# Three tanh operations per head pair instead of four, in score tiles of two and of three PSUM banks, and gate exponentials as powers of e on GpSimd: a fused soft-capped attention and mixture-of-experts attention kernel

## The chip, the cores and the metric

The kernel runs on one core of one Trainium2 chip. The metric is the device time of one execution in microseconds (us); the number quoted for a version is the median of several executions. Beside it there is one profiled execution, from which all views below are taken.

## The reference

Two layers follow each other. The first is ordinary attention with a soft cap on the scores, for 8 batches, 12 heads, 448 tokens and 64 values per head. Its output, rearranged to 448 tokens by 768 features per batch, is the input x of the second layer: four small causal attention experts, of which each token uses the two with the largest gate logits.

```python
# layer 1, per batch and head (S = 448, head size 64, cap = 30)
scores = cap * tanh(q @ k.T / sqrt(64) / cap)
x = softmax(scores) @ v                      # heads side by side: (448, 768)

# layer 2, per batch (E = 4 experts, head size 64, top 2)
logits = x @ w_gate                          # (448, 4)
w = softmax over the two largest logits of each token
for e in range(4):
    a = causal_softmax((x @ wq[e]) @ (x @ wk[e]).T / 8)
    out += w_e * (a @ (x @ wv[e]) @ wo[e])   # only where e is among the two
```

The kernel leaves out the subtraction of the maximum: the cap bounds the scores, and the other exponents are small. Row sums come from a column of ones in v, and division comes after the product with v.

## The kernel before, in words

**Pairs.** Layer 1 is worked off in 48 pairs of heads (`NP`, six per batch). A pair needs, for 448 queries, seven blocks of 128 key rows by 448 query columns: chunk 0 is a block that both heads share (the last 64 keys of each, one head in the upper and one in the lower half of the rows), and chunks 1 to 3 are 128 keys each, once for each head. Seven blocks are 7 x 448 = 3136 columns per pair.

**Scores in PSUM.** A block of 448 f32 columns takes one PSUM bank of 512. The eight banks are split in two pools: `ps_score`, two tiles of two banks each, and `ps_aux`, four tiles of one bank, which everything else on TensorE shares (transposes, the products with v, all projections, the expert outputs). `fill` (L467) writes a score tile with matmuls (L476 for the shared block, L480 for the others, two of which run on half the rows of the array each), and `tanh` (L488) has ScalarE read it into the f16 tile y (L510). `HALF = (1, 2, 2, 2)` says how many blocks each of the four tanh operations of a pair takes. One exponential over all 3136 columns follows per pair (`expo`, L516). The last five pairs of the last batch are worked off in two halves of their tokens ("A" and "B", tiles s0A, s1A, s0B, s1B), so that the second layer of that batch can begin early.

**Second layer.** When the six pairs of a batch are done, its steps are queued: q and k of the experts (L724), v and gate logits (L640, with the copy of the logits at L663), scores (`b_fill`, L762, in the same score tiles), their exponentials on ScalarE (`b_exp`, L781) with the causal mask on GpSimd (L789), the product with v (L808), a transpose (L585), the output projection (L863) and the store (L884). `b_gexp` (L674) is the exponential of the gate logits, 128 x 16 values per batch, on ScalarE; its reader is the product `wun` on VectorE (L688).

**Order.** The list `prog` fixes the order on ScalarE: for a pair, its first tanh (T), the exponential (E) of the pair before, the other tanh operations, and in some slots two expert exponentials (X). `XAT` and `EXPB` say in which slots. All that read a score tile (T and X) are numbered; the fill of read n has to wait for read n - 2, which frees its tile. `Plan` is a planner that runs while the program is being written: it keeps a clock for TensorE, VectorE and ScalarE and a list of free aux banks, and puts the queued steps between the fills, as they become ready and by their due times. What it decides is fixed: each engine then executes its own list in order and waits on semaphores. `keep_warm` adds matmuls without use (L898) in the first 13 slots.

**The end.** `last_batch` takes what the planner has not yet placed, closes the score pool, opens its banks as a second pool for TensorE's outputs, and orders everything that remains with a search over a graph (`Graph`). GpSimd also casts the inputs (L385 to L404) and issues the weight loads; inputs and outputs go through SyncE's queue.

Of the kernel before, what the change touches and what calls it, by code (L numbers as in the profile page):

```python
# [10 lines left out]
f32 = mybir.dt.float32  # L11
f16 = mybir.dt.float16
AF = mybir.ActivationFunctionType
ALU = mybir.AluOpType
# [3 lines left out]
class Plan:  # L18
# [6 lines left out]
    def __init__(self):  # L25
        self.pe = self.dve = self.act = 0.0
        self.done = {}

        self.aux = [0.0] * 4
        self.opened = set()  # L30
        self.work = []

# [207 lines left out]
def kernel(  # L240
# [13 lines left out]
    nc = tc.nc  # L254

    B, H, S, Dh = q.shape
# [17 lines left out]
    xp = ctx.enter_context(tc.tile_pool(name="xp", bufs=2))  # L274
    bp = ctx.enter_context(tc.tile_pool(name="bp", bufs=2))
    outp = ctx.enter_context(tc.tile_pool(name="outp", bufs=8))
    ps_aux = ctx.enter_context(tc.tile_pool(name="ps_aux", bufs=4, space=bass.MemoryType.PSUM))
    scores = ctx.enter_context(ExitStack())
    ps_score = scores.enter_context(
        tc.tile_pool(name="ps_score", bufs=2, space=bass.MemoryType.PSUM)  # L280
    )

    ctx.enter_context(tc.manual_schedule())
# [154 lines left out]

    HALF = (1, 2, 2, 2)


    CUT = 256
# [4 lines left out]
    score = {}  # L449

    def fill_part(u, i):

        p, h = u
        qt, kt = qkt[p]
        x = slice(*TOK[h])
        n = x.stop - x.start
        sc = ps_score.tile([128, 2, 512], f32, name=f"s{i}{h}_{p}", tag="score")
        if i:
            nc.tensor.matmul(sc[:, 0, 0:n], kt[:, 0:128], qt[:, x], start=True, stop=True)
        for c in (2,) if i else (0, 1):  # L460
            for g in range(2):
                r = slice(64 * g, 64 * (g + 1))
                o = n * (1 - g) if i else n * c
                nc.tensor.matmul(
                    sc[:, g, o : o + n], kt[r, 128 * (c + 1) : 128 * (c + 2)], qt[r, x],
                    start=True, stop=True,
                )  # L467
        score[(u, i)] = sc

    def fill(p, i):  # L470
        if isinstance(p, tuple):
            return fill_part(p, i)
        qt, kt = qkt[p]
        sc = ps_score.tile([128, 2, 512], f32, name=f"s{i}_{p}", tag="score")
        if i == 0:
            nc.tensor.matmul(sc[:, 0, 0:S], kt[:, 0:128], qt, start=True, stop=True)  # L476
        else:
            for g in range(2):
                r = slice(64 * g, 64 * (g + 1))
                nc.tensor.matmul(  # L480
                    sc[:, g, 0:S], kt[r, 128 * i : 128 * (i + 1)], qt[r, :],
                    start=True, stop=True,
                )
        score[(p, i)] = sc

    y = {}
# [2 lines left out]
    def tanh(u, i):  # L489
        p, h = u if isinstance(u, tuple) else (u, "")  # L490
        if i == 0:
            y[u] = actp.tile([128, 7 * S], f16, name=f"y{h}_{p}", tag="y", bufs=2)
        sc = score.pop((u, i))
        if not h:
            o, n = sum(HALF[0:i]), HALF[i]
            parts = [(o * S, sc[:, 0:n, 0:S], n)]
        else:
            n = TOK[h][1] - TOK[h][0]
            if i == 0:
                parts = [(0, sc[:, :, 0 : 2 * n], 2)]  # L500
            elif 2 * n == 512:
                parts = [(4 * n, sc.rearrange("p b n -> p (b n)")[:, 0 : 3 * n], 1)]
            else:
                parts = [(4 * n, sc[:, 0, 0 : 2 * n], 1), (6 * n, sc[:, 1, 0:n], 1)]
        for o, src, k in parts:
            w = src.shape[-1]
            dst = y[u][:, o : o + k * w]
            if k > 1 or len(src.shape) > 2:
                dst = dst.rearrange("p (k w) -> p k w", w=w)
            nc.scalar.activation(dst, src, AF.Tanh, scale=isc / capf)  # L510
# [8 lines left out]
    def prob(p, w, j, g):  # L519

        h = "AB"[w >= CUT]
        if (p, h) in pr:
            lo, hi = TOK[h]
            i = (4 if j == 0 else 4 + g + (j == 3) if j > 2 else j - 1 + 2 * g)
            o = (hi - lo) * i + w - lo
            return pr[p, h][:, o : o + 128]
        o = S * (0 if j == 0 else 2 * j - 1 + g) + w
        return pr[p][:, o : o + 128]

    xt = {}  # L530
# [138 lines left out]
    def b_gexp(b, h=""):  # L669
        s = st[b]  # L670
        s["eexp", h] = bp.tile(
            [128, 2 if h else 4, E], f32, name=f"eexp{h}_{b}", tag="eexp", bufs=3
        )
        nc.scalar.activation(s["eexp", h], s["lg", h], AF.Exp)  # L674

    def gate_steps(b, h=""):

# [75 lines left out]
    def b_fill(b, r, g):  # L753
        s = st[b]
        qe = s["qe", r]
        ke = s["ke", r]
        sc = ps_score.tile([128, 1024], f32, name=f"sB{g}_{b}_{r}", tag="score")

        def block(e, o, ko, n, to):

            h = slice(64 * e, 64 * (e + 1))
            nc.tensor.matmul(  # L762
                sc[to : to + n, o : o + S - ko], ke[h, ko : ko + n], qe[h, ko:S], start=True,
                stop=True,
            )
# [192 lines left out]
    def rows(w):  # L958
        return w.rearrange("(c p) m -> p c m", p=128)

    loads = []
    for r in range(2):
        for e in (2 * r, 2 * r + 1):
# [7 lines left out]
        loads += [("o", wo2[e // 2][e % 2 * Dh : (e % 2 + 1) * Dh, :], moe_wo[e])]  # L971


    XAT = [(3, 5)] * 5 + [(2, 4), (2, 3), (3, 4)]
    EXPB = {HP * (b + 1) + o: (b, r) for b in range(B) for r, o in enumerate(XAT[b])}

    prog = []
    for i, u in enumerate(UNITS):  # L980
        t = [("T", u, k) for k in range(2 if isinstance(u, tuple) else 4)]
        e = [("E", UNITS[i - 1])] if i else []
        x = [("X", *EXPB[i], g) for g in range(1 if i >= NP else 2)] if i in EXPB else []
        prog.append(("S", i))
        if i in (1, 2):
            prog += e + t
        elif isinstance(u, tuple):
            prog += t[0:1] + e + x + t[1:]
        else:
            prog += t[0:1] + e + x[0:1] + t[1:2] + x[1:2] + t[2:4]  # L990
    prog += [("S", len(UNITS)), ("E", UNITS[-1])]
    reads = [o for o in prog if o[0] in "TX"]
    where = [i for i, o in enumerate(prog) if o[0] in "TX"]
# [4 lines left out]
    def dur(o):  # L998
        if o[0] == "S":
            return 0.0  # L1000
        if o[0] == "X":
            return 0.7 if o[1] == B - 1 else 0.9
        n = S
        if isinstance(o[1], tuple):
            n = TOK[o[1][1]][1] - TOK[o[1][1]][0]
        if o[0] == "E":
            return 0.08 + 0.00084 * 7 * n
        if n < S:
            return 0.05 + 0.00084 * n * (4, 3)[o[2]] + 0.04 * (o[2] == 1 and n < 256)
        return 0.055 + 0.373 * HALF[o[2]]  # L1010

    def fill_dep(o):
        if o[0] == "T":
# [5 lines left out]
    def do_fill():  # L1019
        nonlocal nfill  # L1020
        o = reads[nfill]
        rel = ends[nfill - 2] + 0.15 if nfill >= 2 else 0.0
        cost = 0.36 if o[0] == "X" or o[2] or isinstance(o[1], tuple) else 0.19
        for d in fill_dep(o):
            plan.force(d)
        at = plan.act + sum(dur(x) for x in prog[pos : where[nfill]])
        rel = max(rel, *(plan.done[d] for d in fill_dep(o)))
        plan.pump(rel, max(rel + 0.05, at - cost - 0.25))
        plan.pe = max(plan.pe, rel) + cost
        if o[0] == "T":  # L1030
# [194 lines left out]


    def l_fill(b, r, _):
        sc = ps_score.tile([128, 2, 512], f32, name=f"sLA_{r}", tag="score")
        o = 0
        for _, k0, q0, q1 in BANKS["A", r][0]:  # L1230
            for e in range(2):
# [8 lines left out]
    def l_exp(b, r, _):  # L1240
# [1 line left out]
        o = BANKS["A", r][1]  # L1242
        dst = pL[:, r, o : o + 768]
        nc.scalar.activation(
            dst.rearrange("p (e n) -> p e n", e=2), st[b].pop(("sc", r))[:, :, 0:384], AF.Exp,
            scale=isc,
        )
        for e in range(2):
# [6 lines left out]
    def last_batch():  # L1255
# [17 lines left out]
        G = Graph(  # L1273
            dict(PE=plan.pe, DVE=plan.dve, ACT=plan.act, SP=plan.act, DMA=plan.act),
            dict(aux=[(0.0, t) for t in plan.aux], tail=[(0.0, t3)] * 4),
        )

        BR, BA, BW, BX = 0.0, 0.0, -5.0, 0.0
# [319 lines left out]
    def gate_exp(wait=False):  # L1598
# [71 lines left out]
```

## Time and profile before

| quantity | value |
|---|---|
| median of 3 executions | 320.8 us (320.77 to 320.8) |
| profiled execution, its own time | 320.99 us |
| span of that execution, first to last instruction | 319.3 us |
| granted TensorE clock, mean | 0.987 |
| ScalarE (ACT) busy | 306.8 us, 96% |
| TensorE (PE) busy | 284.9 us, 89% |
| VectorE (DVE) busy | 216.8 us, 68% |
| GpSimd (POOL) busy | 157.1 us, 49% |

An engine's busy time is the time covered by its instructions. Instructions of ScalarE overlap: the next one begins before the one ahead of it has ended, so the mean duration of a group is longer than the time by which each of them moves the engine on. Waits are named as "who <- whom". Lines such as L510 are lines of the kernel before; in the changed kernel the same statements stand some 20 to 40 lines further down.

### The profile page before, as it was taken

The numbers are of one execution on the slowest core, as the hardware profiler recorded it, in microseconds if no ns is written. First come the engines' busy times: TensorE is split into PE (matmuls) and PEld (weight loads), VectorE is DVE, ScalarE is ACT, GpSimd is POOL, SyncE is SP. The second block draws the span as 40 slices with busy tenths as digits, with TensorE's granted clock in tenths as the row PEclk, the third lists the DMA queues.
The fourth block names the chain that finished last, engine by engine and source line by source line (L and its number), as shares of the span: only waits on it lengthen the run. The fifth ranks groups of instructions, "written<-read, shape, count | busy, mean of one in ns | idle before, by whom it ended". The sixth has DMA issues, their size and how long they took to land.

```text
span 319.3 us, 9111 instructions
## 1 busy us (share of the span) xinstructions
PE 284.9 (89%) x3445; PEld 179.6 (56%) x3445; DVE 216.8 (68%) x762; ACT 306.8 (96%) x312; POOL 157.1 (49%) x480
## 2 busy tenths in 40 slices
PE   7887879988999889997799899997999879989994
PEld 2454445655565655566556564655655655556762
DVE  4444446686686877678866876767856976577574
ACT  3999999999999999999999999999999999999973
POOL 4586999947607299865805386082905200220200
PEclk9999999999999999999999979999899999999999
DMA  7699999999026999576083945586012102020134
GB/s 163 173 216 241 211 225 214 223 216 230 4 101 170 257 243 275 148 214 161 13 242 95 257 95 150 169 218 157 3 52 99 27 2 102 0 77 2 52 123 175
DMA packets 65404, 46.22 MB, mean 145 GB/s; under 512 B 26000, under 2 KB 61968, under 8 KB 65360
## 3 DMA queue, kind: packets, MB, share of 16 engines
q1 hardware_dynamic: 54064, 43.28, 53.0%
q0 software_dynamic: 10512, 1.58, 7.1%
q10 hardware_dynamic: 784, 0.77, 0.8%
q8 instruction: 27, 0.44, 0.6%
q14 instruction: 17, 0.14, 0.2%
HBM read 36.19 MB, written 11.01 MB: 148 GB/s over the span
## 4 chain that ended last, share of the span: by engine, by line
ACT 78%; PE 12%; issue 7%; DMA 1%; DVE 1%; DVEq 0%; POOL 0%; ACTq 0%; POOLq 0%
ACT y L510 36%; ACT p L516 30%; ACT pBs L781 8%; PE wops L863 2%; PE vps L640 2%; DMA qf<-in_q_dram 1%; ACT yB L510 1%; PE pv L550 1%; PE qps L724 1%; ACT yA L510 1%; PE kps L724 1%; PE qkB L1171 1%; ACT pB L516 1%; PE pv L544 1%; ACT pBs L1479 0%
## 5 line engine op out<-in xcount | busy, mean ns | idle before, releaser
L510 ACT ACTIVATE y<-s 128x896 f16<-128x896 f32 (+1 forms) x172 | 135.5, 934 | 0.6 <-PE s L476 0.5
L516 ACT ACTIVATE p<-y 128x3136 f16<-128x3136 f16 x43 | 125.7, 2922 | 0.1
L789 POOL TENSOR_SCALAR_AFFINE_SELECT pBs<-pBs 128x128 f16<-128x128 f16 (+1 forms) x112 | 28.2, 277 | 103.5 <-ACT pBs L781 102.2
L550 PE MATMUL pv<-v16s,p 128*128 128x65 f16 x1032 | 55.0, 194 | 0.0
L480 PE MATMUL s<-qt,kt 64*128 64x448 f16 x258 | 46.5, 362 | 9.0 <-ACT y L510 6.8
L550 PEld LDWEIGHTS <-p 128*128 128x128 f16 x1032 | 46.6, 98 | 3.6 <-issue 0.4
L544 PE MATMUL pv<-vtzs,p 128*128 128x130 f16 x172 | 38.8, 225 | 9.0 <-ACT p L516 6.7
L559 DVE RECIPROCAL rc<-pv 128x4 f32<-128x4 f32 x96 | 17.3, 180 | 38.0 <-PE pv L550 36.8
L563 DVE TENSOR_TENSOR xk<-pv,rc 128x256 f16<-128x256 f32 x96 | 40.7, 424 | 3.2
L370 DVE COPY ob<-wops 128x384 f32<-128x384 f32 (+1 forms) x55 | 30.5, 554 | 6.3 <-PE wops L863 5.7
L544 PEld LDWEIGHTS <-p 128*128 128x128 f16 x172 | 16.7, 97 | 27.7 <-ACT p L516 15.5
L480 PEld LDWEIGHTS <-kt 64*128 64x128 f16 x258 | 15.7, 93 | 28.3 <-issue 21.5
L781 ACT ACTIVATE pBs<-sB 128x960 f16<-128x960 f32 (+1 forms) x28 | 30.9, 1116 | 0.5 <-PE sB L762 0.5
L863 PE MATMUL wops<-wo,oT 128*128 128x384 f16 x128 | 30.4, 327 | 0.6 <-DVE oT L370 0.4
L385 POOL CAST q<-qf 112x512 f16<-112x512 f32 x46 | 28.1, 611 | 4.7 <-DMA qf<-in_q_dram 2.8
L640 PE MATMUL vps<-wvg,xT 128*128 128x260 f16 (+1 forms) x192 | 29.6, 275 | 0.0
L399 POOL CAST v16s<-vf 128x384 f16<-128x384 f32 x48 | 24.4, 507 | 6.0 <-DMA vf<-in_v_dram 3.2
L386 POOL CAST k<-kf 128x384 f16<-128x384 f32 x48 | 24.3, 506 | 3.6 <-DMA kf<-in_k_dram 3.6
L370 DVE COPY xT<-xtp 128x448 f16<-128x448 f16 (+2 forms) x52 | 19.1, 368 | 10.2 <-PE xtp L585 8.8
L404 POOL CAST vtzs<-vtf 64x64 f16<-64x64 f32 x96 | 22.5, 234 | 4.7 <-DMA vtf<-in_v_dram 2.0
L431 DVE COPY qt<-tps 128x384 f16<-128x384 f16 x48 | 16.9, 351 | 8.9 <-PE tps L421 8.5
L391 POOL CAST ktzs<-ktf 64x64 f16<-64x64 f32 x92 | 21.4, 232 | 2.8
(178 smaller groups left out, 544.6 us busy)
## 6 DMA issues: line engine op xcount, KB each, us to landing
qf<-in_q_dram SPq DMA_DIRECT2D x22, 448.0 KB, 6.2
out_dram<-ob SPq DMA_DIRECT2D x23, 384.0 KB, 2.3
kf<-in_k_dram SPq DMA_DIRECT2D x22, 384.0 KB, 6.5
vf<-in_v_dram SPq DMA_DIRECT2D x22, 384.0 KB, 6.1
out_dram<-ob SPq DMA_DIRECT2D x8, 192.0 KB, 2.8
ktf<-in_k_dram SPq DMA_DIRECT2D x44, 32.0 KB, 5.6
vtf<-in_v_dram SPq DMA_DIRECT2D x44, 32.0 KB, 5.4
kf<-in_k_dram SPq DMA_DIRECT2D x4, 192.0 KB, 3.5
```

The source lines that it names most:

```text
L370: (nc.scalar.copy if act else nc.vector.tensor_copy)(dst, src)
L385: eng.tensor_copy(q16, qf.rearrange("p h (c d) -> p c h d", c=QC))
L480: nc.tensor.matmul(sc[:, g, 0:S], kt[r, 128 * i : 128 * (i + 1)], qt[r, :], start=True, stop=True,)
L510: nc.scalar.activation(dst, src, AF.Tanh, scale=isc / capf)
L516: nc.scalar.activation(pt[:, 0:n], y.pop(u)[:, 0:n], AF.Exp, scale=capf)
L544: nc.tensor.matmul(pv[:, n, :, :], prob(p, w, 0, 0), vtz[p % 12], start=(n == 0), stop=False, skip_group_check=True,)
L550: nc.tensor.matmul(pv[:, n, g, :], prob(p, w, j, g), v16[p % 12][:, g, j - 1, :], start=False, stop=(j == KC), skip_group_check=True,)
L563: nc.vector.tensor_tensor(xt[p][:, 2 * i : 2 * i + 2, :, :], pv[:, :, :, 0:Dh], rc.broadcast_to((128, 2, 2, Dh)), ALU.mult,)
L640: nc.tensor.matmul(ps, xT[b][:, j, w : w + 128], wvg[:, j, 0 : ps.shape[1]], start=(j == 0 and first), stop=(j == NDC - 1), skip_group_che ...
L781: nc.scalar.activation(pb[:, o0 : o0 + n], st[b].pop(("sc", r, g))[:, 0:n], AF.Exp, scale=isc)
L789: nc.gpsimd.affine_select(out=blk, in_=blk, compare_op=ALU.is_ge, fill=0.0, base=0, pattern=[[1, n]], channel_multiplier=-1,)
L863: nc.tensor.matmul(ps, st[b]["oT", r][:, w : w + 128], wo2[r][:, f * (D // 2) : (f + 1) * (D // 2)], start=(r == 0), stop=(r == 1),)
```

## The change

1. `ps_aux` gets three banks in place of four, and the planner's list of free aux banks has three entries. The score pool has one tile of two banks and one of three, which are used in turn (`score_tile`), so that it holds five banks.
2. A pair is read in three tanh operations of two or three blocks: the operation with number i covers chunk i + 1 of both heads, and one of them (`TAILAT`) also the shared chunk 0. It is the second one where the pair's first tile is the one of two banks, or where an expert exponential stands in the slot; otherwise the third.
3. In slots in which the first tile is the one of two banks, both expert exponentials stand between the second and third tanh. For batch 6 the second expert scores move by one slot (`XAT`, (2, 3) to (2, 4)).
4. The gate exponentials of batches 0 to 6 become `pow(e, logits)` on GpSimd, with a constant tile `euler`. The planner counts them as done 5 us after they are issued. The two halves of the last batch stay on ScalarE.
5. `last_batch` has five banks in its second pool, and forces one more step to be placed before it.

```diff
-        self.aux = [0.0] * 4
+        self.aux = [0.0] * 3
...
-    ps_aux = ctx.enter_context(tc.tile_pool(name="ps_aux", bufs=4, space=bass.MemoryType.PSUM))
+    ps_aux = ctx.enter_context(tc.tile_pool(name="ps_aux", bufs=3, space=bass.MemoryType.PSUM))
...
-        tc.tile_pool(name="ps_score", bufs=2, space=bass.MemoryType.PSUM)
+        tc.tile_pool(name="ps_score", bufs=1, space=bass.MemoryType.PSUM)
...
-    HALF = (1, 2, 2, 2)
+    TAILAT = {0: 1}
+    nscore = 0
+
+    def score_tile(name):
+        nonlocal nscore
+        i = nscore % 2
+        nscore += 1
+        return ps_score.tile([128, 2 + i, 512], f32, name=name, tag=f"score{i}")
+
+    def chunks(p, i):
+
+        return ([0] if TAILAT[p] == i else []) + [i + 1] * 2
...
-        sc = ps_score.tile([128, 2, 512], f32, name=f"s{i}_{p}", tag="score")
-        if i == 0:
-            nc.tensor.matmul(sc[:, 0, 0:S], kt[:, 0:128], qt, start=True, stop=True)
-        else:
-            for g in range(2):
-                r = slice(64 * g, 64 * (g + 1))
-                nc.tensor.matmul(
-                    sc[:, g, 0:S], kt[r, 128 * i : 128 * (i + 1)], qt[r, :],
-                    start=True, stop=True,
-                )
+        sc = score_tile(f"s{i}_{p}")
+        for n, c in enumerate(chunks(p, i)):
+            if c == 0:
+                nc.tensor.matmul(sc[:, 0, 0:S], kt[:, 0:128], qt, start=True, stop=True)
+                continue
+            g = n % 2 ^ (TAILAT[p] == i)
+            r = slice(64 * g, 64 * (g + 1))
+            nc.tensor.matmul(
+                sc[:, n, 0:S], kt[r, 128 * c : 128 * (c + 1)], qt[r, :],
+                start=True, stop=True,
+            )
...
-        nc.scalar.activation(s["eexp", h], s["lg", h], AF.Exp)
+        if h:
+            nc.scalar.activation(s["eexp", h], s["lg", h], AF.Exp)
+        else:
+            nc.gpsimd.tensor_tensor(s["eexp", h], euler, s["lg", h], ALU.pow)
...
+    euler = const.tile([128, 4, E], f32, name="euler")
+    nc.gpsimd.memset(euler, 2.718281828459045)
...
-    XAT = [(3, 5)] * 5 + [(2, 4), (2, 3), (3, 4)]
+    XAT = [(3, 5)] * 5 + [(2, 4), (2, 4), (3, 4)]
...
-        t = [("T", u, k) for k in range(2 if isinstance(u, tuple) else 4)]
+        t = [("T", u, k) for k in range(2 if isinstance(u, tuple) else 3)]
...
+        big = nread % 2
+        nread += len(t + x)
...
+        elif big:
+            prog += t[0:1] + e + x[0:1] + t[1:2] + x[1:2] + t[2:3]
         else:
-            prog += t[0:1] + e + x[0:1] + t[1:2] + x[1:2] + t[2:4]
+            prog += t[0:1] + e + t[1:2] + x + t[2:3]
+        if not isinstance(u, tuple):
+            TAILAT[u] = 2 if big and not x else 1
...
-        return 0.055 + 0.373 * HALF[o[2]]
+        return 0.055 + 0.373 * len(chunks(o[1], o[2]))
...
-        cost = 0.36 if o[0] == "X" or o[2] or isinstance(o[1], tuple) else 0.19
+        cost = 0.36
+        if o[0] == "T" and not isinstance(o[1], tuple) and TAILAT[o[1]] == o[2]:
+            cost += 0.19
...
-        for k in [("v", c, 3), *[("k", c, r) for r in range(2)], ("vl", 0), *plan.opened]:
+        for k in [("v", c, 3), ("xt", p - 3, "B"), *[("k", c, r) for r in range(2)], ("vl", 0), *plan.opened]:
...
-            tc.tile_pool(name="ps_tail", bufs=4, space=bass.MemoryType.PSUM)
+            tc.tile_pool(name="ps_tail", bufs=5, space=bass.MemoryType.PSUM)
...
-            plan.act = max(plan.act, d) + 0.1
-            plan.done[("G", ngate)] = plan.act + plan.LAT
+            if ngate < B - 1:
+                plan.done[("G", ngate)] = max(plan.act, d) + 5.0
+            else:
+                plan.act = max(plan.act, d) + 0.1
+                plan.done[("G", ngate)] = plan.act + plan.LAT
```

More of the change, by code (lines that the diff above doesn't have):

```diff
@@ L437, in a_tr, with y_of @@
         qkt[p] = (qt, kt)
-    HALF = (1, 2, 2, 2)
+    TAILAT = {0: 1}
[7 more added lines that the diff above has]
+        return ([0] if TAILAT[p] == i else []) + [i + 1] * 2
+    def y_of(p, j):
+        if j == 0:
+            return 2 * TAILAT[p]
+        return 2 * (j - 1) + (TAILAT[p] <= j - 1)
     CUT = 256
@@ L456, in fill_part @@
         n = x.stop - x.start
-        sc = ps_score.tile([128, 2, 512], f32, name=f"s{i}{h}_{p}", tag="score")
+        sc = score_tile(f"s{i}{h}_{p}")
         if i:
@@ L494, in tanh @@
         if not h:
-            o, n = sum(HALF[0:i]), HALF[i]
+            cs = chunks(p, i)
+            o, n = y_of(p, cs[0]), len(cs)
             parts = [(o * S, sc[:, 0:n, 0:S], n)]
@@ L499, in tanh @@
             if i == 0:
-                parts = [(0, sc[:, :, 0 : 2 * n], 2)]
+                parts = [(0, sc[:, 0:2, 0 : 2 * n], 2)]
             elif 2 * n == 512:
@@ L526, in prob @@
             return pr[p, h][:, o : o + 128]
-        o = S * (0 if j == 0 else 2 * j - 1 + g) + w
+        o = S * (y_of(p, j) + g) + w
         return pr[p][:, o : o + 128]
@@ L756, in b_fill @@
         ke = s["ke", r]
-        sc = ps_score.tile([128, 1024], f32, name=f"sB{g}_{b}_{r}", tag="score")
+        sc = score_tile(f"sB{g}_{b}_{r}").rearrange("p b n -> p (b n)")
         def block(e, o, ko, n, to):
@@ L971 @@
         loads += [("o", wo2[e // 2][e % 2 * Dh : (e % 2 + 1) * Dh, :], moe_wo[e])]
-    XAT = [(3, 5)] * 5 + [(2, 4), (2, 3), (3, 4)]
+    XAT = [(3, 5)] * 5 + [(2, 4), (2, 4), (3, 4)]
     EXPB = {HP * (b + 1) + o: (b, r) for b in range(B) for r, o in enumerate(XAT[b])}
     prog = []
+    nread = 0
     for i, u in enumerate(UNITS):
-        t = [("T", u, k) for k in range(2 if isinstance(u, tuple) else 4)]
+        t = [("T", u, k) for k in range(2 if isinstance(u, tuple) else 3)]
         e = [("E", UNITS[i - 1])] if i else []
         x = [("X", *EXPB[i], g) for g in range(1 if i >= NP else 2)] if i in EXPB else []
+        big = nread % 2
+        nread += len(t + x)
         prog.append(("S", i))
@@ L1227, in l_fill @@
     def l_fill(b, r, _):
-        sc = ps_score.tile([128, 2, 512], f32, name=f"sLA_{r}", tag="score")
+        sc = score_tile(f"sLA_{r}")
         o = 0
@@ L1244, in l_exp @@
         nc.scalar.activation(
-            dst.rearrange("p (e n) -> p e n", e=2), st[b].pop(("sc", r))[:, :, 0:384], AF.Exp,
+            dst.rearrange("p (e n) -> p e n", e=2), st[b].pop(("sc", r))[:, 0:2, 0:384], AF.Exp,
             scale=isc,
@@ L1274, in last_batch @@
             dict(PE=plan.pe, DVE=plan.dve, ACT=plan.act, SP=plan.act, DMA=plan.act),
-            dict(aux=[(0.0, t) for t in plan.aux], tail=[(0.0, t3)] * 4),
+            dict(aux=[(0.0, t) for t in plan.aux], tail=[(0.0, t3)] * 5),
         )
```

## The prediction

> **What bounds the kernel now.** I read the page's busy times first, then the waits of ScalarE, the chain of waits in order of time, the groups of ScalarE by form, the windows, and last TensorE's timeline at the end.
>
> ```profile
> PE 284.9 (89%) x3445; PEld 179.6 (56%) x3445; DVE 216.8 (68%) x762; ACT 306.8 (96%) x312; POOL 157.1 (49%) x480
> ACT 78%; PE 12%; issue 7%; DMA 1%; DVE 1%; DVEq 0%; POOL 0%; ACTq 0%; POOLq 0%
> ```
>
> ```profile
> ACT y L510 <- PE s L476: 0.5, 1, 0.5
> ACT pBs L781 <- PE sB L762: 0.5, 1, 0.5
> ```
>
> ScalarE is the bound of the long middle part: from the first tanh to the last it waits twice for a score tile, 0.5 us each. The chain shows what one pair costs there (start, length):
>
> ```profile
> 24.80 2.86 ACT y L510 x4
> 27.66 2.70 ACT p L516
> 30.36 2.86 ACT y L510 x4
> ...
> 59.25 0.81 ACT y L510
> 60.06 0.92 ACT pBs L781
> 60.97 2.05 ACT y L510 x3
> 63.03 2.70 ACT p L516
> 65.83 2.85 ACT y L510 x4
> ```
>
> A pair takes 2.86 + 2.70 = 5.56 us. A tanh of 896 columns moves ScalarE on by 0.81 us; three of which one has 448 columns take 2.05, so the short one takes 0.43. Between 63.03 + 2.70 and 65.83 lies 0.10 us: there ScalarE runs one gate exponential. The groups by form give longer means, since neighbours overlap:
>
> ```profile
> L516 ACT ACTIVATE p<-y 128x3136 f16<-128x3136 f16 x43 | 125.7, 2922 | 0.1
> L510 ACT ACTIVATE y<-s 128x896 f16<-128x896 f32 x129 | 116.5, 1029 | 0.0
> L510 ACT ACTIVATE y<-s 128x448 f16<-128x448 f32 x43 | 27.9, 648 | 0.6 <-PE s L476 0.5
> L674 ACT ACTIVATE eexp<-lg 128x16 f32<-128x16 f32 x7 | 2.2, 319 | 0.0
> ```
>
> The end is another stage. In the windows (length, then busy time of PE, PEld, DVE, ACT, POOL) ScalarE's share falls only in the last, while TensorE is nearly full from 260 us on:
>
> ```profile
> 240.00:260.00 20.00, 17.76 (x244) 12.12 (x245) 16.76 (x63) 20.00 (x21) 5.64 (x21) 1.00 0.15 51
> 260.00:280.00 20.00, 18.83 (x213) 11.32 (x210) 12.20 (x34) 19.55 (x19) 2.27 (x10) 1.00 0.12 47
> 280.00:295.00 15.00, 14.02 (x197) 8.59 (x194) 12.20 (x47) 15.00 (x20) 1.85 (x9) 1.00 0.11 33
> 295.00:319.00 24.00, 19.32 (x261) 13.43 (x260) 13.70 (x55) 17.65 (x36) 1.68 (x5) 0.98 0.32 116
> ```
>
> TensorE's timeline there (start, length, a bracket where it idled before) runs almost without a gap from the last score fill (s1B, 299.72) to the last projections:
>
> ```profile
> 297.33 1.15 PE L640 MATMUL vps<-wvg,xT 128*128 128x256 f16 x9
> 298.42 0.34 PE L464 MATMUL s0B<-qt,kt 64*128 64x192 f16 x4
> ...
> 299.40 0.45 PE L1213 MATMUL lgA<-wvg,xT 128*128 128x4 f16 x12
> 299.72 0.24 PE L459 MATMUL s1B<-qt,kt 128*128 128x192 f16 x1
> ...
> 304.57 0.81 PE L863 MATMUL wops<-wo,oT 128*128 128x384 f16 x4
> 305.22 0.25 PE L1171 MATMUL qkB<-xT,wq 128*128 128x192 f16 x1
> ...
> 313.82 1.48 PE L863 MATMUL wops<-wo,oT 128*128 128x384 f16 x8 [0.22 <-ACT oT L370]
> ```
>
> So what ScalarE saves in the middle counts in full only if TensorE brings no more work into this end.
>
> **Tanh operations.** 43 pairs lose one operation each; the columns stay. By end-to-end times in the trace (medians) a tanh of 448 columns costs 437 ns and one of 896 costs 810: 373 ns for 448 columns, so 64 ns per operation that do not depend on length. One of 1344 is then 1.18 us where 0.44 + 0.81 = 1.25 stood. Gain 43 x 0.064 = 2.7 us, on the bounding engine; if the exponential's 2.70 against four tanh at 2.86 is used, 0.16 / 3 = 0.053 each, 2.3 us.
>
> A rule stands against reading it so small. The Trainium skill, "ScalarE: Activation LUTs", section "What ACT_TABLE_LOAD costs", gives 280 ns + 0.833 ns per column where the bias is a pointer, and an overlap of about 93 ns back to back. The group means (648 and 1029 ns) fit the first half. By the second half a removed operation would bring 187 ns, 8.0 us in all; the chain, in which four take 2.86 us, speaks for an overlap of some 215, and I go by the chain.
>
> **Gate exponentials.** Seven at 0.10 us leave ScalarE: 0.7 us. What comes in their place is a GpSimd operation on 128 x 16 f32 that no row shows. Nearest rows: the memset of 128x12 at 0.15 us, the mask selection of 128x128 at 0.29, the 128x512 cast at 0.61, a DMA issue at 0.97. I take 0.15 to 1.0 us, nearest the casts. In GpSimd's order each stands behind the casts of a pair, which the timeline shows running ahead of ScalarE, and before the mask selections that wait for ScalarE anyway (102 us of GpSimd's idle time). Its reader on VectorE, `wun`, is planned 5 us after the issue, where the old trace had 65.6 to 68.4, 2.8 us. So at 1 us it is hidden with room to spare: cost nothing. Without that cover, `wun` holds VectorE's queue (evacuations of the aux banks), TensorE runs out of banks, then fills are late.
>
> The Trainium skill, "GPSIMD Engine Reference", section "Instruction dispatch", says that the first call of a freshly loaded routine also pays about 6 us without a visible instruction. No run here shows it; by it the first of the seven would be late by 1 to 2 us, once.
>
> **Fills.** The fill of a pair's first tile has to fit between the end of the second-last tanh and that of the last. It was one matmul of 448 columns in 0.81 us; it is two that share the array (0.36 us for the pair of L480, as long as the one of L476), in 0.81 or 1.18. Nothing lost; the second tight place per pair goes. The 0.45 us wait before the batch 6 exponentials at 278.70 lies where `XAT` moves them; I count nothing for it, up to 0.45 gain in the range.
>
> **Three aux banks.** From the trace, with TensorE's matmuls put beside their order in the program, each aux tile gets its first write and last read. Between 100 and 260 us four banks are held 9% of the time, three 33%. Of the 438 openings, 63 before 300 us find three others held; kept in that order they would have to wait 2.0 + 3.9 + 10.5 + 4.7 = 21 us together (to 60, 160, 265, 300 us). The planner reorders instead, so most is not waited but moved later. How much, the two programs' orders show: after the last score fill (s1B of pair 47) TensorE has 223 matmuls instead of 196. The 27 are 9 of v (298.42 - 297.33 = 1.09 us), the 12 of the gate logits (299.72 - 299.40 = 0.32), 4 of the projection (305.22 - 304.57 = 0.65) and 2 transposes (0.11): 2.2 us more in the stage that TensorE fills. Of it 0.8 us may fall into the gaps that this stage shows (0.39 + 0.19 + 0.22). So the end grows by 1.4 to 2.2 us; I take 2.0. Eight `keep_warm` matmuls fewer save nothing: they stand before 100 us, in idle time.
>
> For waits that the planner does not foresee, I put 0.3 us (bounds 0, and 3.5: a sixth of the 21 us).
>
> **Sum**, against the profiled execution (320.99, span 319.3): -2.7 - 0.7 + 2.0 + 0.3 = -1.1, about 319.9 us; the median of the runs is 0.2 lower, so the forecast is 319.7 us. With the terms' own bounds: -3.4 + 1.4 - 0.45 = -2.4 (318.4), and -3.0 + 2.2 + 0.6 = -0.2 (320.6).
>
> **Rivals.**
> - *More is kept:* the graph search for the end hides the extra TensorE work in more than the gaps above, because that stage is a chain of dependences (x to q/k to scores to product to projection) as much as full. For it: VectorE is idle over 10 of the last 24 us. Against: hardly any TensorE gap is left. Time 320.8 - 3.4 + 0.5 = 317.9, up to the forecast's edge at 318.6. Chance 0.14.
> - *Eaten at the end:* 2.2 us more there and 0.5 to 1.5 us of bank waits, within 0.2% (0.64 us, about what a measurement of this kernel can tell from no change) of 320.8: 320.2 to 321.4. Chance 0.20.
> - *Bank waits decide (slower):* with three banks a VectorE delay reaches TensorE one step sooner; its place is the batch steps, 31 of the 63 openings at 160 to 265 us. It turns the sign once more than 1.4 us of the 21 is lost beyond the plan (one fifteenth), and is measurable from 2.0. At 3.5 us the time is 320.8 - 3.4 + 2.0 + 3.5 = 322.9. Against: the planner knows of the three banks, and what it gave up for them is already counted as the work moved to the end. Chance 0.18.
> - *The power is slow:* if it takes over 5 us, `wun` is late in seven batches. At 6 us, 7 x 1 = 7 us, less a few tenths of cover each: 319.7 + 5 = 325 or more. Chance 0.08.
>
> **How the numbers follow.** Forecast 0.40, for 318.6 to 320.2. Faster by over 0.2%: 0.40 + 0.14 = 0.54; within: 0.20; slower: 0.18 + 0.08 = 0.26. The range goes from 318.0, which leaves out the far part of the first rival (0.05), to 322.5, which leaves out the slow power and the far part of the bank waits (0.12). The likeliest case alone is 318.6 to 320.2.
>
> **What would show it.** Right: 43 tanh of 1344 columns with 1.18 us end to end, pairs of 5.50 us, the last exponential of pair 47 ended near 300.2 us instead of 303.6, and from there to the end of the span some 2 us more than the old 15.7. Wrong: waits of y for s summing to over 2 us in ScalarE's list, `wun` waiting for GpSimd, or a power row above 5 us. The forecast falls if the last exponential ends no earlier than 302 us, or if the last stage does not grow.

## The result, and the profile after

| | median, us | runs | ratio to the kernel before, 95% interval |
|---|---|---|---|
| kernel before, first set | 320.8 | 5 | |
| changed kernel, first set | 320.46 (320.14 to 320.52) | 5 | 0.9982 [0.9967, 0.9997] |
| changed kernel, again on another chip | 320.01 (before there: 320.9) | 9 | 0.997 [0.9958, 0.9981] |

The changed kernel is 0.3 to 0.9 us faster by the medians, 0.2 to 0.3% by the ratios. The forecast was 1.1 us: the first set's 320.46 us lies outside its likeliest case (318.6 to 320.2), the second set's gain of 0.9 us inside. Executions at a granted clock of 0.85 or less (one of the run that counts a store as 1.44 us, two of the kernel before beside it) are left out of all medians, ratios and readings below. The profiled execution took 320.46 us, its span 318.7 us (319.3 before).

The page of the changed kernel: ScalarE's busy time fell little, and its share of the chain fell from 78 to 57%, since the chain now also runs through TensorE, GpSimd and DMA.

```profile
PE 285.2 (89%) x3437; PEld 175.0 (55%) x3437; DVE 218.3 (68%) x759; ACT 304.2 (95%) x265; POOL 177.7 (56%) x488
ACT 57%; PE 20%; issue 6%; POOL 5%; DMA 4%; DVE 4%; SPq 1%; DVEq 0%; POOLq 0%; ACTq 0%
```

Its chain in order of time, in the middle (start, length):

```profile
44.20 2.71 ACT p L538
...
49.69 2.71 ACT p L538
...
55.19 2.71 ACT p L538
57.90 0.86 ACT pBs L806
58.76 1.18 ACT y L532
```

From one exponential to the next a pair takes 5.49 and 5.50 us, where 5.56 stood, and a tanh of 1344 columns moves ScalarE on by 1.18 us: both as forecast. ScalarE's waits for score tiles stay small:

```profile
ACT y L532 <- PE s L501: 1.1, 3, 0.5
ACT yA L532 <- PE s0A L484: 0.2, 1, 0.2
```

The last exponential of pair 47 ends at 300.49 us instead of 303.63: 3.1 us gained. What became of them shows in two stretches behind it. The first reaches to the last copy of an output (ob, L370). Its window before and after (the columns are length, then busy time of PE, PEld, DVE, ACT, POOL):

```profile
303.63:315.99 12.36, 10.86 (x139) 7.42 (x136) 8.90 (x38) 9.05 (x21) 0.00 (x0) 1.00 0.39 145
```

```profile
300.49:314.14 13.65, 12.62 (x160) 8.89 (x158) 10.20 (x44) 9.84 (x25) 0.00 (x0) 1.00 0.37 135
```

TensorE has 1.76 us more to do there, its idle time shrinks from 1.50 to 1.03, and the stretch is 1.29 us longer. The second stretch is that from the last copy to the end of the span: 3.28 us before, 4.60 after, 1.32 us more. So 3.1 - 1.3 - 1.3 leaves the 0.5 us by which the span is shorter. The timelines show the end of the kernel before, and then of the changed kernel:

```profile
314.84 1.15 DVE L370 COPY ob<-wops 128x384 f32<-128x384 f32 x2 [0.90 <-PE wops L863]
315.43 1.13 ACTq L884 DMA_DIRECT2D out_dram<-ob  x2
```

```profile
312.21 2.55 SPq L909 DMA_DIRECT2D out_dram<-ob  x4
...
313.12 1.02 DVE L370 COPY ob<-wops 128x384 f32<-128x384 f32 x2 [0.50 <-PE wops L888]
313.46 1.19 ACTq L909 DMA_DIRECT2D out_dram<-ob  x2
```

The changed kernel issues its last store at 314.17 us, 1.86 earlier than the kernel before (316.03), but that store lands 3.65 us after its issue, where 2.32 were enough before (landings by the same traces).

The power on GpSimd takes 2.9 us, every time:

```profile
L699 POOL TENSOR_TENSOR eexp<-euler,lg 128x16 f32<-128x16 f32 x7 | 20.3, 2906 | 2.0 <-DVE lg L685 1.6
```

### The profile page after: what moved, and what is told of

It is laid out like the page before. It is cut to its first block, busy times and chain, and to the rows that moved or that the text cites. A ratio compares the mean times of both kernels' runs of the same rounds, so it can differ in the third digit from the quotient of the medians.

```text
span 318.7 us, 9085 instructions
## 1 busy us (share of the span) xinstructions
PE 285.2 (89%) x3437; PEld 175.0 (55%) x3437; DVE 218.3 (68%) x759; ACT 304.2 (95%) x265; POOL 177.7 (56%) x488
## 4 chain that ended last, share of the span: by engine, by line
ACT 57%; PE 20%; issue 6%; POOL 5%; DMA 4%; DVE 4%; SPq 1%; DVEq 0%; POOLq 0%; ACTq 0%
ACT y L532 25%; ACT p L538 24%; ACT pBs L806 5%; DMA vf<-in_v_dram 3%; PE pv L572 2%; PE wops L888 2%; PE vps L662 2%; PE kps L749 1%; PE s L501 1%; PE dummy L923 1%; PE qps L749 1%; DMA vtf<-in_v_dram 1%; PE sB L787 1%; PE pv L566 1%; POOL k L386 1%
## 5 line engine op out<-in xcount | busy, mean ns | idle before, releaser
L532 ACT ACTIVATE y<-s 128x896 f16<-128x896 f32 x129 | 131.8, 1135 | 1.1 <-PE s L501 1.1
L370 DVE COPY ob<-wops 128x384 f32<-128x384 f32 (+1 forms) x54 | 29.7, 553 | 7.5 <-PE wops L888 7.3
L501 PEld LDWEIGHTS <-kt 64*128 64x128 f16 x258 | 14.6, 93 | 33.3 <-issue 27.0
L806 ACT ACTIVATE pBs<-sB 128x960 f16<-128x960 f32 (+1 forms) x28 | 30.1, 1094 | 0.1
L370 DVE COPY xT<-xtp 128x448 f16<-128x448 f16 (+2 forms) x52 | 19.1, 368 | 8.7 <-PE xtp L607 7.0
```

What stands on the lines that cost most here:

```text
L370: (nc.scalar.copy if act else nc.vector.tensor_copy)(dst, src)
L501: nc.tensor.matmul(sc[:, n, 0:S], kt[r, 128 * c : 128 * (c + 1)], qt[r, :], start=True, stop=True,)
L806: nc.scalar.activation(pb[:, o0 : o0 + n], st[b].pop(("sc", r, g))[:, 0:n], AF.Exp, scale=isc)
```

## The experiments

**Theory "end":** ScalarE's gain is real, and the end of the kernel takes most of it back, through TensorE's backlog and the stores. Rivals: the power costs time ("power"), or the third bank costs waits in the middle ("bank waits").

The stages of each profiled execution (us; "E" is the last exponential of pair 47):

| kernel | first tanh to E | E to last copy | TensorE busy in it | last copy to end | span |
|---|---|---|---|---|---|
| before | 296.3 | 12.37 | 10.86 | 3.28 | 319.3 |
| changed | 293.3 | 13.65 | 12.62 | 4.60 | 318.7 |
| changed, again | 293.4 | 13.66 | 12.62 | 4.49 | 318.5 |
| exp on ScalarE | 295.0 | 13.57 | 11.97 | 3.87 | 319.5 |
| power alone | 295.9 | 12.99 | 11.31 | 4.28 | 320.3 |
| three banks alone | 298.2 | 13.58 | 12.07 | 4.24 | 322.8 |
| power twice | 292.9 | 13.66 | 12.62 | 4.27 | 317.7 |
| before without batch 6 projection | 296.7 | 10.83 | 9.00 | 3.85 | 318.7 |
| changed without it | 293.3 | 12.60 | 10.75 | 4.07 | 317.1 |

The profiles of "exp on ScalarE" and "three banks alone" hold one wait of 1.73 and 1.49 us near 16 us that the others do not have, so their column "first tanh to E" is that much longer.

### The gate exponentials back on ScalarE

```diff
-        if h:
-            nc.scalar.activation(s["eexp", h], s["lg", h], AF.Exp)
-        else:
-            nc.gpsimd.tensor_tensor(s["eexp", h], euler, s["lg", h], ALU.pow)
+        nc.scalar.activation(s["eexp", h], s["lg", h], AF.Exp)
```

(The planner's time for them is as in the kernel before, too.)

> The changed kernel with the gate exponentials back on ScalarE (three banks and three tanh kept). Theory 'end' (ScalarE's gain is real, and the TensorE work and stores at the end take it back): the last exponential of pair 47 ends some 0.7 us later than in the changed kernel (about 301.2 us), but TensorE has 215 matmuls after the last score fill instead of 223, so the time is within 0.4 us of the changed kernel's, 320.2 to 320.9 us. Rival 'power' (the power on GpSimd costs time through VectorE or GpSimd): faster than the changed kernel by over 0.4 us, below 320.0.

Measured: 319.64 us (319.49 to 321.23), ratio 0.9962 [0.995, 0.9975]. The time is below the 320.2 to 320.9 that the theory gave. Without the power the rest of the change gives the whole gain; the changed kernel's own 0.997 [0.9958, 0.9981] does not lie below it. The numbers fit "power" as they stand (319.64 is below 320.0), but that bound was set for the first chip, and the run with the doubled power, on the same chip, speaks against: 319.68. So in the changed kernel the power neither helps nor hurts measurably. The last exponential came at 302.07, not at 301.2: this profile, of the slowest of the seven executions (321.23 us), has a wait of 1.73 us near 16 us, of which the section on the hardware tells.

### The power alone

```diff
-        nc.scalar.activation(s["eexp", h], s["lg", h], AF.Exp)
+        if h:
+            nc.scalar.activation(s["eexp", h], s["lg", h], AF.Exp)
+        else:
+            nc.gpsimd.tensor_tensor(s["eexp", h], euler, s["lg", h], ALU.pow)
```

(The planner counts them as done after 5 us, as in the changed kernel.)

> The kernel before with only the gate exponentials of batches 0 to 6 moved to GpSimd (four tanh, four aux banks). Theory 'end': the last exponential ends 0.7 us earlier (about 302.9), 15 more matmuls of v and gate logits stand after the last score fill (some 0.7 us), so no change: 320.4 to 321.1 us. Rival 'power': slower than before by over 0.4 us, above 321.2. If ScalarE's 0.7 us counts in full: 320.1.

Measured: 321.99 us (321.48 to 323.81) against 320.7, ratio 1.0039 [0.9998, 1.0080]: 1.3 us slower by the medians, above the theory's 320.4 to 321.1, with an interval that just reaches no change. The last exponential ends at 302.99, 0.64 us earlier, as expected. The stretch behind it grew by 0.62 us with 0.45 more of TensorE, and the last copy fell at the same time as before (315.99). The stores then took 1.0 us longer. The expectation had the first part right and lacked the second. The time is in the range of "power" (above 321.2), but `wun` never waited for GpSimd, so the delay that this rival names is not in the trace.

### Three aux banks alone

```diff
-        self.aux = [0.0] * 4
+        self.aux = [0.0] * 3
...
-    ps_aux = ctx.enter_context(tc.tile_pool(name="ps_aux", bufs=4, space=bass.MemoryType.PSUM))
+    ps_aux = ctx.enter_context(tc.tile_pool(name="ps_aux", bufs=3, space=bass.MemoryType.PSUM))
```

(With five banks in the end's pool and the one forced step, as in the changed kernel.)

> The kernel before with three aux banks in the middle instead of four, one bank of PSUM left unused there, four tanh kept; the pool of the end has five banks as in the changed kernel. Theory 'end': ScalarE hardly waits more (last exponential at 303.3 to 304.2 us), 18 more matmuls stand after the last score fill (some 1.05 us), so slower by 0.5 to 1.5 us: 321.3 to 322.3. Rival 'bank waits': ScalarE waits for score fills by over 1.5 us more in the middle, last exponential after 305 us, time above 322.5.

Measured: 323.54 us (322.34 to 324.68), ratio 1.0087 [1.0065, 1.0108]: slower by 2.8 us, more than either bound of the theory and in the rival's range. The last exponential ended at 304.94, just below the rival's 305. ScalarE's list of waits and its timeline:

```profile
ACT y L510 <- PE s L480: 1.6, 2, 1.5
ACT y L510 <- PE s L476: 0.5, 1, 0.5
ACT pBs L781 <- PE sB L762: 0.4, 1, 0.4
```

```profile
15.33 1.74 ACT L510 ACTIVATE y<-s 128x896 f16<-128x896 f32 x2 [1.49 <-PE s L480]
```

Between the first tanh and the last exponential ScalarE idled 2.42 us, where it was 0.69 before. One wait of 1.49 us follows a stretch at half TensorE clock (11.3 to 14.7 us), and 0.38 us lie in a second one (from 147.9 us); the remaining 0.55 are no more than before. So the waits that "bank waits" asked for are there, nearly at its bound, but all that is new of them stands at or behind a fall of the clock. The stretch behind the last exponential grew by 1.21 us with 1.21 more of TensorE, and the end by 0.96. The power alone, with four banks, has 1.0 us more at its end too, so only the 1.21 can be laid to the missing bank. The three tanh operations pay for it: between this kernel and the one with exp on ScalarE lie the tanh operations and the moved expert scores, and there the last exponential ends 2.87 us earlier (302.07), near the 2.7 forecast for the tanh operations; the ratios, 1.0087 and 0.9962, are 4 us apart.

### The power twice

```diff
+            t = bp.tile([128, 4, E], f32, name=f"eone_{b}", tag="eone", bufs=3)
+            nc.gpsimd.tensor_tensor(t, euler, s["lg", h], ALU.pow)
             nc.gpsimd.tensor_tensor(s["eexp", h], euler, s["lg", h], ALU.pow)
```

> The changed kernel with each power computed twice on GpSimd (the first into a tile that nobody reads), so 5.8 us stand where 2.9 stood, against the planner's 5 us. Theory 'end': the one power is hidden with over 1 us to spare, and the doubled one makes wun late by about 1 us in some batches, which aux banks absorb in part: 0 to 2 us slower than the changed kernel, 320.4 to 322.5, with wun now waiting for GpSimd in the list of waits. Rival 'power' (already the single one is on the path): at least 2.9 us slower per batch, 7 x 2.9 = 20 us in all, 335 to 341.

Measured: 319.68 us (319.4 to 320.16), ratio 0.9967 [0.9954, 0.998]: like the changed kernel. Of seven readers one waited, 0.6 us:

```profile
DVE wun L715 <- POOL eexp L701: 0.6, 1, 0.6
```

Hidden with more room than I had given it, and "power" is off by 15 us.

### The changed kernel once more

> The changed kernel itself once more, beside the kernel before on the chip of this set. Its doubled-power variant, in which every engine but GpSimd has the same list, gave 319.68 against 320.70. Theory 'power is hidden': the same ratio here, 0.995 to 0.998. Rival 'the power helps or hurts with the load of GpSimd': a ratio outside of that.

Measured: 320.01 us (319.45 to 320.4), ratio 0.997 [0.9958, 0.9981], as the first theory said.

### Both kernels without batch 6's output projection

```diff
-                plan.add(("wo", b, n, f), 0.33, 0.5, d, due, b_wo, b, n, f)
+                if b != B - 2:
+                    plan.add(("wo", b, n, f), 0.33, 0.5, d, due, b_wo, b, n, f)
```

> The kernel before without batch 6's output projection and its stores (left out, so batch 6 of the output is not written). 12 of TensorE's matmuls of that projection, 2.0 us, stood after the last score fill. Theory 'TensorE's backlog fills the end': the last stage from the end of the last exponential shrinks by 1 to 2 us. Rival 'chain of dependences': the end does not depend on filling work, less than 0.5 us.

> The changed kernel without batch 6's output projection and its stores (left out, so batch 6 of the output is not written). 16 such matmuls, 2.6 us, stood after the last score fill. Theory 'TensorE's backlog': the last stage shrinks by 1.5 to 2.6 us, and against the kernel before with the same cut this one is faster by 1.2 to 2.5 us, where the whole kernels differ by 0.3 to 1.0. Rival 'chain of dependences': the two cut kernels differ by as little as the whole ones.

Measured: 319.83 us (319.49 to 322.22), ratio 0.9974 [0.9957, 0.9991], and 318.23 us (317.77 to 318.84), ratio 0.9914 [0.9899, 0.993]. The cut kernels differ by 1.6 us, the whole ones in the same set by 0.9. The windows from the last exponential to the last copy, of the kernel before and of the changed kernel, both cut:

```profile
303.98:314.81 10.83, 9.00 (x116) 5.99 (x116) 7.51 (x31) 6.35 (x16) 0.00 (x0) 1.00 0.19 74
```

```profile
300.39:312.98 12.59, 10.75 (x148) 7.54 (x148) 8.59 (x42) 7.49 (x20) 0.00 (x0) 1.00 0.17 64
```

Either loses 1.86 us of TensorE's work, and the stretch shrinks by 1.54 and 1.05 (I had expected 1.5 at least for the second). It depends on filling work, so "chain of dependences" alone is wrong. Against the kernel before, the stretch grew by nearly as much as TensorE's work in it with three banks alone (1.21 and 1.21 us), with exp on ScalarE (1.20 and 1.11) and with the power alone (0.62 and 0.45); in the changed kernel it grew by 1.29 for 1.76.

In the whole kernels, what is added there is mostly output projection. The same windows, for the instructions on the tile wops alone (length, then PE, DVE, ACT), before and after:

```profile
303.63:315.99 12.36, 4.92 (x25) 2.79 (x5) 4.29 (x9) 1.00 0.39 145
```

```profile
300.49:314.14 13.65, 7.07 (x32) 3.14 (x6) 4.58 (x10) 1.00 0.37 135
```

Yet batch 6's projection is not needed for the difference: with it cut from both, 16 matmuls of the projection are left in either, and the stretches still differ by 1.77 us, with 1.75 of TensorE. What is added is then q and k of the last batch's second half (12 matmuls more), its gate logits (6) and products with v of the first half (12). So no single step makes the two kernels differ: when the last exponential ends, TensorE is behind by about the same amount, whatever steps stand last in its list. That the two cut kernels differ by more than the whole ones comes mostly from the table's column "last copy to end", where they are 0.22 us apart instead of 1.32.

### Stores left out

Batch 6's four stores left out, in the changed kernel:

```diff
     def b_store(b, n, fs=(0, 1), act=False):
+        if b == B - 2:
+            return
```

> The changed kernel with all of batch 6's projection computed and copied, but its four stores left out (batch 6 of the output is not written). Theory 'stores crowd the end': in the changed kernel the last store landed 3.65 us after its issue where the kernel before had 2.32; without the four others it lands after 2.3 to 3.0 us, so 0.5 to 1.3 us faster than the changed kernel. Rival 'the last stores are late by their own order (a 128-row half is issued last)': 3.2 us or more remain, time as the changed kernel's within 0.4 us.

Measured: 320.55 us (319.58 to 321.88), ratio 0.9989 [0.9975, 1.0003]. The last store landed 3.76 us after its issue, as the rival said; the time is 0.5 us above the changed kernel's in the same set, a little outside the rival's 0.4 and away from the theory's 0.5 to 1.3 below. So batch 6's stores are not what makes the last store late.

The two full stores of the last batch left out (`if b == B - 1 and n < 2`):

> The changed kernel with the two full stores of the last batch's first half of rows left out (they are computed and copied, rows 0 to 255 of the last batch are not written). Theory 'drain' (the time from the issue of the first of the last six stores to the landing of the last is 5.3 to 5.7 us in every profile so far, set by their 1.18 MB): only 0.59 MB remain, the last store lands 2.3 to 2.9 us after its issue instead of 3.55 to 3.65, so the time is 0.7 to 1.3 us below the changed kernel's (320.0 on the chip of the last set): 318.7 to 319.4. Rival 'the last store is slow by itself' (its rows, its queue): no change, 319.7 to 320.4.

Measured: 319.97 us (319.25 to 320.3), ratio 0.9958 [0.9943, 0.9974]. The last store landed 3.23 us after its issue, and the ratio is lower than the changed kernel's by 0.0012, with overlapping intervals. The time lies in the rival's range, and the landing misses the theory's 2.3 to 2.9. Four profiles with the same order of the end and these stores in place (the changed kernel twice, the power twice, batch 6's stores left out) had 3.33 to 3.77, so leaving out 0.79 MB of the last 1.38 is worth some tenths of a microsecond at most. (The expectation's 1.18 MB is wrong, and in the changed kernel without batch 6's projection the six stores took 6.4 us, not 5.3 to 5.7.)

### Another order of the end

The search counts a full store as 1.44 us instead of 1.0, so that it issues the last batch's first rows earlier:

```diff
-                kb = max(0.5, 0.5 * len(fs) * (0.5 if n == 3 else 1.0))
+                kb = 0.72 * len(fs) * (0.6 if n == 3 else 1.0)
```

> The changed kernel, in which the search for the order of the end counts a store as 1.44 us on the DMA queue instead of 1.0 (halves 0.72 and 0.43 instead of 0.5); nothing else differs. Its order issues the first of the last six stores some 0.9 us earlier, relative to the other work of the end. Theory 'drain': the end follows the first of the six, 0.3 to 1.0 us below the changed kernel: 319.0 to 319.7. Rival 'compute sets the end': the last copies come 0.15 us later, so 0 to 0.3 us above it.

Measured: 319.91 us (319.67 to 320.51), ratio 0.9961 [0.9947, 0.9976], against 321.2 for the kernel before in that set: not to be told from the changed kernel. There is no profile to read beside the others. The same with 0.85 in place of 0.72:

> As the run with a store counted as 1.44 us, with 1.7 us (halves 0.85 and 0.51): the first two of the six come earlier still (1.7 us earlier than in the changed kernel), the last copies some 0.3 us later. Theory 'drain': the last four stores meet an empty queue and land 2.3 to 2.9 us after issue: 318.8 to 319.6. Rival 'compute sets the end': 0.2 to 0.6 us above the changed kernel.

Measured: 320.39 us (319.94 to 321.68), ratio 0.9978 [0.9966, 0.9991]. The first of the last six stores left at 310.84, 1.4 us earlier than in the changed kernel, the last copies came 0.35 us later after the last exponential, and the last store landed 3.15 us after its issue. What the stores gained, the copies lost, as the rival had it.

At last, the small halves after the larger ones, as the kernel before happened to have them:

```diff
-                    [("wo", b, n, f, 2) for f in fs], b_store, b, n, fs,
+                    [("wo", b, n, f, 2) for f in fs]
+                    + [("st", b, 2, (k,)) for k in (0, 1) if last and n == 3], b_store, b, n, fs,
```

> The changed kernel with one more rule for the search at the end: the two halves of the last 64 rows are stored after the two halves of the 128 rows before them, the order that the kernel before had by chance (SyncE, ScalarE, SyncE, ScalarE). Theory 'order of the last four': the last four stores take 3.2 to 3.5 us from the first issue to the last landing, as in the kernel before (3.17), instead of 4.26 to 4.36 in the changed kernel, so 0.6 to 1.2 us below the changed kernel, ratio to the kernel before 0.993 to 0.996. Rival 'bytes alone' (the queue drains at one rate, whatever the order): 3.9 to 4.4 us, ratio 0.996 to 0.999.

Measured: 319.77 us (319.18 to 321.3), ratio 0.996 [0.9946, 0.9975]. The last four stores took 4.36 us from the first issue (312.61) to the last landing (316.97), as long as in the changed kernel. The rival held in the trace, though its ratio lies at the edge between the two. But the edit restored the order of the sizes alone: the four left on ScalarE, SyncE, SyncE, ScalarE, and not on SyncE, ScalarE, SyncE, ScalarE as in the kernel before. The order of the two queues was therefore not tested.

So no version here is clearly better than the changed kernel; the one with exp on ScalarE (0.9962) needs neither the power nor GpSimd's 20 us.

## Why the prediction was right, and where it was off

- **Tanh operations:** forecast 2.7 us for 43 of them, 64 ns each; measured 5.50 us per pair instead of 5.56, and 1.18 us for 1344 columns. Right, and the two runs with three banks and ScalarE's exponentials say nearly the same (2.87 us). The rule of the Trainium skill ("ScalarE: Activation LUTs", "What ACT_TABLE_LOAD costs": an overlap of about 93 ns) would have made it 187 ns; the trace decides against it.
- **Gate exponentials:** forecast 0.7 us on ScalarE; the power alone brought the last exponential 0.64 us forward. Right there. The bounds of the power's own length (0.15 to 1.0 us) were too low by nearly a factor of three at the least: it took 2.90. The step that failed is taking the nearest GpSimd rows, which are casts, memsets and selections, as bounds for a power of 16 columns. The reason given for a cost of nothing held all the same: `wun` came 2.0 us or more after the power's end in each batch, and even 5.8 us were hidden but for one 0.6 us.
- **The first call:** the Trainium skill's 6 us for a freshly loaded routine ("GPSIMD Engine Reference", "Instruction dispatch") did not show: the seven powers took 2898 to 2937 ns, and the first ran from 64.8 to 67.8 us like the others, right behind casts that lasted until 64.74.
- **Three banks:** forecast 2.0 us at the end by 2.2 us more of TensorE, 0.8 of it in gaps, bounds 1.4 to 2.2. Measured: 1.76 us more in the stretch behind the last exponential, 0.47 in gaps, so 1.3 us. The mechanism was right, the size somewhat below the lower bound. The 27 matmuls were counted rightly (196 and 223 behind the last score fill), but TensorE's busy time from there to the last copy grew by 1.45 us (14.29 to 15.74), not by 2.2: the prediction added lengths of rows, and neighbouring matmuls overlap (in the changed kernel one of 0.25 us starts at 298.40 and the next at 298.49). The v and the logits that it counted had run before the last exponential ended; what they pushed behind it is projection, q and k.
- **Waits beyond the plan:** forecast 0.3 us; between the first tanh and the last exponential ScalarE idled 0.99 us instead of 0.69. Right. (Of the two waits of 0.5 us that the prediction read in the kernel before, one stands ahead of the first tanh, at 7.3 us; and its upper sum takes 0.6 us of waits where the stated bound was 3.5.)
- **Missing term:** the sum ended at the last copy. The stores behind it cost 1.3 us more than before. From the last exponential to the end of the span, where the prediction expected "some 2 us more than the old 15.7", 2.6 us were added (15.64 to 18.25). Two errors partly cancel here, which is luck: the stretch to the last copy was put 0.7 us too high, the stores were left out. Together they turn the forecast's 1.1 into the 0.5 of the profiles.
- **Rivals:** the first set's 320.46 us lies in the range of "eaten at the end" (0.20; 320.2 to 321.4), with the stores in the place of its bank waits. "The power is slow" needed over 5 us; it took 2.9. "Bank waits decide" was not what happened, but a missing bank alone costs 2.8 us, more than the 2.3 that the sum held.

**What stays open:** why the last stores take longer. In the profiles of the kernel before, 2.32 us pass from the last issue to its landing, in the changed kernel and its variants 2.9 to 3.8. Batch 6's stores are not it (3.76 without them), and the two full ones of the last batch are some tenths at most. The order of the queues is open. In the five profiles in which the last four stores left on SyncE, ScalarE, SyncE, ScalarE they took 3.17 to 3.88 us from the first issue to the last landing; in the eight in which the first left on ScalarE, 3.93 to 4.47. No run was made to test this, the orders of sizes and the gaps to the stores ahead differ too, and the profile that was left out does not follow it (ScalarE first, 3.33 us). Whether the kernel before, with one profile, is the exception could not be settled.

## To carry to other kernels

Take the gain of a faster bounding engine at the place where that engine stops being the bound, and then follow what is left up to the landing of the last store, not to the last copy: here 3.1 us became 1.8 and then 0.5. A fixed order that was planned around a resource (PSUM banks) moves work to the end when the resource shrinks, and the number of instructions behind the last critical one shows the direction before any run (the sum of their lengths overstated it here, 2.2 us for 1.45). An operation without a row should be bounded by what its kind may cost, not by the nearest other kind; but what decides is the slack of its reader, and doubling the operation measures that slack directly.

## What the runs showed of the hardware

- A power on GpSimd with 128 x 16 f32 values takes 2.90 us (seven of seven within 2898 to 2937 ns), ten times a mask selection of 128x128 (0.29 us). Divided by its 16 columns that is 181 ns; only this size was run.
- The granted TensorE clock falls to 0.5 for 3.41 us at a time, none to twice per execution before the end, at different places: at 184.9 and 222.4 us in the kernel before, at 114.9 and 190.0 in the changed one, at 11.3 and 147.9 in the three-bank kernel, at 11.5 in the one with exp on ScalarE. Two falls of one profile lie whole multiples of 3.41 us apart (37.55, 75.09 and 136.54 us: 11, 22 and 40 times). In the 3.41 us ahead of each of the 17 falls in the profiles read here, TensorE was busy for only 0.49 to 0.58 of the time, far less than its 89% of the span. The changed kernel's window ahead of its first fall, and that of the fall (length, then PE, PEld, DVE, ACT, POOL, then the clock):

```profile
111.53:114.94 3.41, 1.78 (x33) 1.27 (x32) 2.52 (x10) 3.41 (x3) 3.16 (x9) 1.00 1.12 262
114.94:118.36 3.42, 3.42 (x48) 2.47 (x46) 2.35 (x9) 3.42 (x4) 3.05 (x11) 0.50 1.11 255
```

Not every such window is followed by a fall (0.52 from 186.4 us in the changed kernel's second profile, and none behind it), so the share alone does not decide. In the middle, waits of ScalarE of up to 0.5 us follow within 8 us of the end of such a fall, and behind some falls there is none; behind the two near the start stand the 1.49 and 1.73 us. That the fall is the cause rests on this order in time.
- The changed kernel's five executions of the first set had granted clocks of 0.986 to 0.991 and took 320.14 to 320.52 us. In the second set three at 0.985 to 0.991 took 320.23 to 320.40, and six at 0.994 to 0.998 took 319.45 to 320.20. Part of the difference between the two sets may be that.
- Five profiles with the same lists on ScalarE, VectorE and TensorE (the changed kernel twice, the power twice, the two with stores left out) took 292.76 to 293.36 us from the first tanh to the last exponential, with 0.42 to 1.15 us of waits of ScalarE. The power twice had no fall of the clock before the end (292.85), the run without the two full stores had one (292.76). So differences of 0.6 us between single profiles need no other cause, and the number of falls does not order them.
